# Turning two tensors on the matrix engine, keeping off-diagonal blocks on chip, and moving short transfers to ScalarE's queue, in a recurrent-attention and MLP kernel

## Chip, core and metric

The kernel runs on one core of a Trainium2 chip. Its engines have instruction streams of their own: TensorE (PE in the profile, PEld for its weight loads), VectorE (DVE), ScalarE (ACT), GpSimd (POOL) and SyncE (SP). SP here only issues DMA transfers. The metric is the device time of one execution in microseconds.

## The reference

A recurrence over 768 steps (4 batches of 8 heads, state 40x40), and two MLP layers on its result:

```python
for t in range(S):
    y[:, :, t] = np.einsum('bhd,bhde->bhe', rt, state)
    Sa = np.einsum('bhde,bhe->bhd', state, at)
    state_decay = state * wt[:, :, None, :] - np.einsum('bhd,bhe->bhde', Sa, bt)
    state = state_decay + np.einsum('bhd,bhe->bhde', vt, kt)
...
h = np.maximum(xt @ w_tok1, 0.0) @ w_tok2          # over tokens
u = x + h.transpose(0, 2, 1)
x = u + np.maximum(u @ w_ch1, 0.0) @ w_ch2         # over channels
...
ch = np.maximum(xn @ w_ch1, 0.0) @ w_ch2           # second layer, xn = layer-normed x
out = x + ch
```

MLP weights come in as float64 and are decoded from their bits on the chip.

## The kernel before

The 768 steps of a batch are cut into 12 chunks of 64. There are 48 chunks in all; two neighbours make a *pair* (24 pairs, `gi`), eight make a *group* (6 groups, `G`). Every fp32 value is split into a high and a low fp16 part, so a product is three matmuls (`T3`).

For each group the background steps are: `stack` loads b, a, k, v, r (tile `x`), scales them by running products of w (`sx`, `wf`), writes the two fp16 parts into `o16` (one buffer for all tensors and groups; ACT at L785, DVE or POOL at L789 and L787) and stores it to DRAM (`scr_*`, L704). `gram_load` (L809) reads a and b back by DMA transposes into `at` and `tt_b`, four of each in a group. `gram` multiplies them (L826); the diagonal 32x32 blocks go to `sab` and DRAM `l_d` (L836), the off-diagonal ones as high and low part to `lc` (L833, L834) and DRAM `o_d` (L838). `solve` reads `l_d` back as `ug` (L843), inverts 32x32 triangles by 60 dependent DVE steps (L853, L855), and stores the result `u16` to DRAM `t_d` (L867).

For each pair `pair_load` fetches k, v, r transposed (L926), rows (L929), and `tu` from `t_d` (L941). `low_load` fetches the off-diagonal blocks into `lx`, one 64-row buffer whose other half holds zeros (L951). `early` makes the scores of k and a, masks them, and forms the inverse's lower block: 48 matmuls of `lx` with `tu`, their result back into `lx`, then 48 more (L995). `chain` (twice for a pair) is the recurrence; it cannot start on a pair before `early` of it is done. `yout_a` and `yout_b` form the outputs. `split_mask` masks a 128x512 PSUM tile on DVE into SBUF (`se`, `sm`, L958), makes the high part on ACT (L961) and the low one on POOL (L962).

Weights: 56 pieces are loaded (`raw`, three buffers, L1135), decoded by four DVE steps (L1137 to L1144), scaled and split by ACT (L1159, L1162), and their low part formed by POOL (L1163). The MLP of a batch (L1240 token product; L1289, L1292 and L1299 channel products, L1246 and L1247 the split between them) can start when all 12 chunks of the batch are through.

The order on each engine is no hand's work: `fix_order` lists all instructions, simulates them with costs (`cost`, `mode`, `LAG`) and fixes the resulting order engine by engine. All DMAs stand in SP's queue.

Of the kernel before, what the change touches and what calls it, by code (L numbers as in the profile page):

```python
# [195 lines left out]
STAY = 1500  # L196
CLOCK = 4096 / 1.2
# [3 lines left out]
def cost(i, engine):  # L201
# [17 lines left out]
    if "Dma" in kind or "DMA" in kind:  # L219
# [5 lines left out]
        return 625 if len(rows) > 1 or 64 in rows or turned else 450, size / piece * (9 + piece / 27) / k  # L225
# [29 lines left out]
class Graph:  # L255
# [114 lines left out]
    def latest(self, key):  # L370
# [16 lines left out]
        while events:  # L387
# [5 lines left out]
            for e in engines:  # L393
# [4 lines left out]
                if move:  # L398
                    dma = max(now, dma) + move
                    begin[x] = dma + 650 + own  # L400
                    busy[e] = max(now + own + 25 + (545 if self.turns(x) else 0), dma - 1500)
                else:
                    begin[x] = busy[e] = now + own
# [11 lines left out]
    def schedule(self, rank):  # L415
# [22 lines left out]
        issue = dma = 0  # L438
        warm, window, active, tiles = False, 0, 0.0, 0
        port = dict(DVE=0, Pool=0)  # L440
        order = {e: [] for e in engines}
        events = [(0, 0, x) for x in range(n) if not wait[x]]
        heapq.heapify(events)
        while events:
# [7 lines left out]
            for e in engines:  # L452
# [35 lines left out]
                if move:  # L488
                    begin = max(now + 100, issue)
                    issue = begin + own + 25  # L490
                    dma = end = max(begin + own + 650, dma) + move
                    busy[e] = begin + own - 75 + (620 if self.turns(pick) else 0) if e == "SP" else begin + 900
# [49 lines left out]
def tile_main(  # L542
# [86 lines left out]
    lx = const.tile([128, 8, 2, 64], F16, name="lx")  # L629
# [33 lines left out]
    def zero_rings():  # L663
        for ring in (tt_r, [lx], n16_r, [zero]):
# [8 lines left out]
    l_d, t_d, o_d = {}, {}, {}  # L673
    for G in range(NG // TG):
# [5 lines left out]
        o_d[G] = dr.tile([2, 32, TG * NPAIR, 64], F16, name=f"o_d{G}")  # L680
# [25 lines left out]
    def pre_steps(G):  # L706
# [64 lines left out]
        def stack(n, src, e):  # L771
# [19 lines left out]
            store_lanes(scr[n, G], o16)  # L791
# [6 lines left out]
    def t_steps(G):  # L798
        TU = 8

        st_i = {}

# [9 lines left out]
        def gram(i):  # L812
            st = st_i[i]
            if G == 0:
                lc = chp.tile([128, TU, 2, 32], F16, name="lc", tag="sak", bufs=2)
                sab = chp.tile([128, TU, 32], F32, name="sab", tag="sm", bufs=2)
            else:
                lc = pre.tile([128, TU, 2, 32], F16, name="lc")
                sab = pre.tile([128, TU, 32], F32, name="sab")
            for j in range(TU // 4):  # L820
# [15 lines left out]
            nc.sync.dma_start(out=l_d[G].rearrange("(u l) t -> l u t", l=128)[:, TU * i:TU * i + TU, :], in_=sab)  # L836
            for h2 in range(2):
                nc.sync.dma_start(out=o_d[G][h2][:, TU * i:TU * i + TU, :],  # L838
                                  in_=lc[64 * h2:64 * h2 + 32].rearrange("p u r t -> p u (r t)"))

        def solve():
            ug = pre.tile([128, 32, 32], F32, name="ug")
            nc.sync.dma_start(out=ug.rearrange("p s t -> p (s t)"),  # L843
# [13 lines left out]
            for s0 in range(0, 32, 8):  # L857
# [9 lines left out]
                nc.sync.dma_start(out=dv[:, s0:s0 + 8, :], in_=u16.rearrange("p s r t -> p s (r t)"))  # L867
# [7 lines left out]

        return dict(gram=load + steps, solve=[solve])
# [42 lines left out]
    def pair_load(gi, late):  # L919
# [553 lines left out]
```

## Time and profile before

| | us |
|---|---|
| median of three runs | 1201.86 (1199.35 to 1214.21) |
| the profiled execution | 1205.77 |
| its span in the trace, first to last instruction | 1204.1 |

[...] A queue name with q (SPq) is the issuing part of an engine. "Idle before" is the idle time of an engine ahead of an instruction, with what ended it.

### The profile page before, as it was taken

Reading aid. Unit: us, or ns where it says so; the run is one execution under the profiler, and the core shown is the slowest. Engines: PE = TensorE matmul, PEld = TensorE weight load, DVE = VectorE, ACT = ScalarE, POOL = GpSimd, SP = SyncE. Lnnn points to the kernel's source line nnn. Section 1 sums busy time; section 2 is a strip of 40 time slices with the busy share of each in tenths; the row PEclk is TensorE's granted clock in tenths of the full one; section 3 lists DMA queues with packets and bytes.
Section 4 is the critical chain, followed back from the end, with each engine's and each line's share of the span. In section 5 each row is a group of like instructions: output and inputs, shape, how many; then the busy total and the mean of one; then the engine's idle time right before and its main releaser. Section 6 shows DMA issues by size and latency. Waiting matters only on the chain.

```text
span 1204.1 us, 37444 instructions
## 1 busy us (share of the span) xinstructions
PE 870.2 (72%) x15950; PEld 702.5 (58%) x15950; DVE 735.2 (61%) x1769; ACT 614.8 (51%) x1425; POOL 341.8 (28%) x340
## 2 busy tenths in 40 slices
PE   0010000456768668898989999889899999999997
PEld 0010000445657556676767777667778877788875
DVE  6866578678855774667854579536854453434432
ACT  1462228756777355853567634585474453332221
POOL 2765553552225522072231143121111001100000
PEclk9999999999999578998989999889999999999999
DMA  4899999797995899879899657977475554222111
GB/s 153 222 240 233 189 210 254 199 193 163 198 194 121 207 170 217 114 146 128 169 197 142 147 81 177 166 149 173 97 131 87 72 71 77 35 42 38 27 25 26
DMA packets 401726, 170.95 MB, mean 142 GB/s; under 512 B 370576, under 2 KB 381328, under 8 KB 397712
## 3 DMA queue, kind: packets, MB, share of 16 engines
q1 hardware_dynamic: 401552, 168.48, 70.2%
q8 instruction: 127, 2.08, 0.7%
q14 instruction: 47, 0.39, 0.1%
HBM read 73.27 MB, written 54.26 MB: 106 GB/s over the span
## 4 chain that ended last, share of the span: by engine, by line
PE 37%; ACT 8%; DVE 8%; DMA 7%; issue 3%; POOL 1%; SPq 1%; POOLq 0%; ACTq 0%; DVEq 0%
PE pb L1299 12%; PE pa L1289 10%; PE ch L907 4%; PE pa L1292 3%; PE ps L907 3%; DMA ut<-u 2%; DVE ug L855 2%; ACT sab L829 1%; ACT tt L987 1%; DMA t_d<-u 1%; DVE hh L1247 1%; DVE tmp L853 1%; PE ps L1240 1%; PE ps L995 1%; ACT o L785 1%
## 5 line engine op out<-in xcount | busy, mean ns | idle before, releaser
L1299 PE MATMUL pb<-c,hh 128*128 128x320 f16 x864 | 183.3, 301 | 1.2 <-DVE hh L1247 1.1
L1289 PE MATMUL pa<-ut,c 128*128 128x256 f16 x864 | 169.4, 283 | 8.9 <-DVE hh L1247 4.4
L1247 DVE SCALAR_TENSOR_TENSOR hh<-pa,hh 128x512 f16<-128x512 f32 x132 | 90.5, 687 | 138.4 <-ACT hh L1246 138.1
L1299 PEld LDWEIGHTS <-hh 128*128 128x128 f16 x1584 | 153.1, 99 | 33.1 <-DVE hh L1247 1.6
L1246 ACT ACTIVATE hh<-pa 128x512 f16<-128x512 f32 x132 | 78.3, 594 | 162.4 <-PE pa L1292 159.8
L1299 PE MATMUL pb<-d,hh 128*128 128x320 f16 x720 | 151.8, 306 | 0.0
L1289 PE MATMUL pa<-ut,d 128*128 128x256 f16 x720 | 141.1, 281 | 5.4 <-DMA ut<-u 4.4
L962 POOL TENSOR_TENSOR srx<-sm,srx 128x512 f16<-128x512 f32 x48 | 56.7, 1182 | 285.0 <-ACT srx L961 281.8
L1289 PEld LDWEIGHTS <-c 128*128 128x128 f16 x864 | 86.2, 102 | 30.9 <-issue 4.6
L1289 PEld LDWEIGHTS <-d 128*128 128x128 f16 x720 | 70.9, 101 | 25.8 <-DMA ut<-u 3.4
L855 DVE TENSOR_TENSOR ug<-ug,tmp 128x30 f32<-128x30 f32 (+9 forms) x180 | 83.7, 465 | 1.6
L995 PE MATMUL ps<-tu,lx 64*64 64x32 f16 x2304 | 65.2, 190 | 26.2 <-DMA lx<-o_d 8.2
L785 ACT ACTIVATE o<-x 128x2560 f16<-128x2560 f32 x30 | 70.0, 2332 | 26.3 <-POOL x L712 17.3
L853 DVE TENSOR_TENSOR tmp<-ug 128x30 f32<-128x30 f32 (+9 forms) x180 | 81.3, 451 | 1.9
L826 PEld LDWEIGHTS <-tt_b 120*128 120x128 f16 x192 | 15.4, 117 | 111.5 <-issue 47.4
L826 PE MATMUL pa<-at,tt_b 120*128 120x128 f16 x64 | 8.2, 308 | 98.0 <-DMA at<-scr_a 39.1
L995 PEld LDWEIGHTS <-lx 64*64 64x64 f16 x2304 | 57.8, 123 | 34.4 <-issue 19.3
L1292 PE MATMUL pa<-ut,c1t 128*128 128x256 f16 x288 | 67.7, 281 | 0.0
L987 ACT ACTIVATE tt<-tu 32x512 f16<-32x512 f16 x96 | 60.1, 626 | 13.3 <-PE ch L907 10.7
L907 PEld LDWEIGHTS <-srx 64*64 64x64 f16 x2304 | 57.6, 121 | 13.8 <-issue 11.5
L1325 POOL TENSOR_TENSOR y<-ve,mhalf 128x2 f32<-128x2 f32 x12 | 9.0, 747 | 181.2 <-DVE ve L1323 123.6
L1140 DVE TENSOR_SCALAR wst<-raw 128x320 int32<-128x320 int32 (+2 forms) x56 | 33.9, 608 | 43.4 <-DMA raw<-in_moe_w_ch_dram 32.2
(195 smaller groups left out, 2031.8 us busy)
## 6 DMA issues: line engine op xcount, KB each, us to landing
raw<-in_moe_w_ch_dram SPq DMA_DIRECT2D x30, 320.0 KB
scr_b<-o SPq DMA_DIRECT2D x6, 1024.0 KB
scr_a<-o SPq DMA_DIRECT2D x6, 1024.0 KB
scr_k<-o SPq DMA_DIRECT2D x6, 1024.0 KB
scr_v<-o SPq DMA_DIRECT2D x6, 1024.0 KB
scr_r<-o SPq DMA_DIRECT2D x6, 1024.0 KB
t_d<-u SPq DMA_DIRECT2D x24, 256.0 KB
tu<-t_d SPq DMA_DIRECT2D x24, 256.0 KB
```

Source lines behind the costliest of these rows:

```text
L785: A.activation(out=hi2, in_=x.unsqueeze(2).broadcast_to([128, HC, 2, D]), func=ACTF.Copy, scale=p2(e))
L853: V.tensor_tensor(out=tv, in0=ug[:, 0:s, s:s + 1].broadcast_to([128, s, n]), in1=ug[:, s:s + 1, s + 1:32].broadcast_to([128, s, n]), op=AL ...
L855: V.tensor_tensor(out=ug[:, 0:s, s + 1:32], in0=ug[:, 0:s, s + 1:32], in1=tv, op=ALU.add)
L907: m = nc.tensor.matmul(out, lhsT, rhs, start=start, stop=stop, skip_group_check=True)
L962: P.tensor_tensor(out=o[:, 1], in0=sm, in1=o[:, 0], op=ALU.subtract)
L987: A.activation(out=tt[l0:l0 + 32, :, :, l0 % 64:l0 % 64 + 32], in_=d["tc"][l0:l0 + 32], func=ACTF.Copy)
L995: nc.tensor.matmul(pv[hs, u, :], lw[hs, u, l, :], rhs[hs, u, m, :], start=n == 0, stop=n == 2)
L1246: nc.scalar.activation(out=hi, in_=ps, func=ACTF.Relu)
L1247: nc.vector.scalar_tensor_tensor(out=lo, in0=ps, scalar=0.0, in1=hi, op0=ALU.max, op1=ALU.subtract)
L1289: nc.tensor.matmul(o, w1[:, f, l, ms], ut[:, f + 3 * q, :], start=n == 0, stop=False)
L1292: nc.tensor.matmul(o, w1t[:, ms], ut[:, 2 + 3 * q, :], start=False, stop=q == 1)
L1299: nc.tensor.matmul(pb[i][:, 0:DM], hh[:, l, c0:c0 + 128], w2[:, m0 + s, q, :], start=m0 + s == 0 and n == 0, stop=m0 + s == nm - 1 and n == 2)
```

## The change

For groups 0 and 1 a and b are no longer read back by DMA transposes: a new step `turn` turns `o16` on PE (32 transposes of 128x120 for each tensor), and ACT and DVE copy the result, eight copies each, into `at` and, for b, into the weight tile `d2`, which is not yet in use. a of these groups is not stored at all. `lc` gets six buffers and is read directly by `early`, so that `o_d`, `lx` and `low_load` are gone; the two rounds of matmuls work on 32x32 tiles. The transfers of `l_d`, `ug`, `t_d` and `tu` (78 in all) are issued by ACT. `split_mask` masks in place in PSUM, and DVE makes the low part. The low part of decoded weights is made by DVE too. Planner: two queues, dearer transposes, a class for 32x32 tiles, and a rule that waits for more urgent work, with limits of zero.

```diff
+WAIT, GAP = 0, 0
-    return (rows <= 64) + 2 * (cols <= 64)
+    return (rows <= 64) + (rows <= 32) + 3 * ((cols <= 64) + (cols <= 32))
...
-    lx = const.tile([128, 8, 2, 64], F16, name="lx")
+    zx = const.tile([128, 8, 2, 32], F16, name="zx")
...
-            store_lanes(scr[n, G], o16)
+            if n != "a" or G > 1:
+                store_lanes(scr[n, G], o16)
...
+        def turn(n):
+            dst = []
+            for i in range(4):
+                st = st_i.setdefault(i, {})
+                if n == "a":
+                    st[n] = stk.tile([128, TU * 128], F16, name="at", bufs=NA)
+                    st_t.setdefault(4 * G + i, {})["a"] = st[n]
+                else:
+                    st[n] = wt["d2"].rearrange("p m l c -> p (m l c)")[:, i * TU * 128:(i + 1) * TU * 128]
+                dst.append(st[n][0:120].rearrange("p (l t) -> p t l", t=HC))
+            for t0 in range(0, HC, 8):
+                pt = ps_b.tile([128, 1024], F16, name="pb", tag="b")[0:120]
+                for t in range(8):
+                    nc.tensor.transpose(pt[:, t * 128:(t + 1) * 128], o16[:, t0 + t, 0:120], ident)
+                pv = pt.rearrange("p (t l) -> p t l", l=128)
+                for i in range(4):
+                    if i % 2:
+                        V.tensor_copy(dst[i][:, t0:t0 + 8], pv[:, :, 32 * i:32 * i + 32])
+                    else:
+                        A.activation(out=dst[i][:, t0:t0 + 8], in_=pv[:, :, 32 * i:32 * i + 32], func=ACTF.Copy)
...
-            nc.sync.dma_start(out=l_d[G].rearrange("(u l) t -> l u t", l=128)[:, TU * i:TU * i + TU, :], in_=sab)
-            for h2 in range(2):
-                nc.sync.dma_start(out=o_d[G][h2][:, TU * i:TU * i + TU, :],
-                                  in_=lc[64 * h2:64 * h2 + 32].rearrange("p u r t -> p u (r t)"))
+            A.dma_start(out=l_d[G].rearrange("(u l) t -> l u t", l=128)[:, TU * i:TU * i + TU, :], in_=sab)
...
     def split_mask(ps, tag, bufs):
-        own = tag == "sak"
-        sm = chp.tile([128, 8, 64], F32, name="se" if own else "sm", bufs=1 if own else 2)
-        V.tensor_tensor(out=sm, in0=ps.rearrange("p (u t) -> p u t", t=64),
-                        in1=causal.unsqueeze(1).broadcast_to([128, 8, 64]), op=ALU.mult)
+        sm = ps.rearrange("p (u t) -> p u t", t=64)
+        V.tensor_tensor(out=sm, in0=sm, in1=causal.unsqueeze(1).broadcast_to([128, 8, 64]), op=ALU.mult)
         o = chp.tile([128, 2, 8, 64], F16, name=tag, bufs=bufs)
         A.activation(out=o[:, 0], in_=sm, func=ACTF.Copy)
-        P.tensor_tensor(out=o[:, 1], in0=sm, in1=o[:, 0], op=ALU.subtract)
+        V.tensor_tensor(out=o[:, 1], in0=sm, in1=o[:, 0], op=ALU.subtract)
...
-        for k, (rhs, dst, sc, rows) in enumerate(((d["uc"], lw, p2(-E_T), 32), (d["tc"], tt, p2(-E_LO), 0))):
+        for k, (lhs, rhs, dst, sc, r0, c0) in enumerate(((d["lc"], d["uc"], zx, p2(-E_T), 0, 0),
+                                                         (zx, d["tc"], tt, p2(-E_LO), 32, 32))):
...
-                    for h2 in range(2):
-                        hs = slice(64 * h2, 64 * h2 + 64)
-                        nc.tensor.matmul(pv[hs, u, :], lw[hs, u, l, :], rhs[hs, u, m, :], start=n == 0, stop=n == 2)
+                    for p0 in (0, 64):
+                        ks, os = (slice(p0 + r, p0 + r + 32) for r in (r0, 32 - r0))
+                        nc.tensor.matmul(pv[os, u, :], lhs[ks, u, l, :], rhs[ks, u, m, :], start=n == 0, stop=n == 2)
...
-            P.tensor_tensor(out=lo, in0=f[p0:128], in1=hi[p0:128], op=ALU.subtract)
+            V.tensor_tensor(out=lo, in0=f[p0:128], in1=hi[p0:128], op=ALU.subtract)
...
-    run(bg(0, "w")[1:] + bg(0, "b a"))
+    run(bg(0, "w")[1:] + bg(0, "b tb a ta"))
```

The new order on SP's queue at the opening, from the store of group 0's b to the store of its k. Before (`scr_b`, `scr_a`, `scr_k` are DRAM copies of `o16`, `raw` are weights):

```order
L704 DMA scr_b_121<-o_118 128x4096
...
L809 DMA_TRANSPOSE tt_b<-scr_b_121 128x1024 x2
L1135 DMA raw<-in_moe_w_tok_dram 128x768
L938 DMA yw<-scr_y_124 128x8x40
L701 DMA wf<-in_w_dram 64x1x1280
L704 DMA scr_a_119<-o_118 128x4096
L701 DMA x<-in_r_dram 64x1x1280
...
L809 DMA_TRANSPOSE at<-scr_a_119 128x1024 x2
L701 DMA x<-in_r_dram 64x1x1280
L809 DMA_TRANSPOSE at<-scr_a_119 128x1024
```

Now, on the same queue:

```order
L722 DMA scr_b_121<-o_118 128x4096
L719 DMA x<-in_k_dram 64x1x1280
L722 DMA scr_y_124<-wf 128x1280
L719 DMA x<-in_k_dram 64x1x1280
L1165 DMA raw<-in_moe_w_tok_dram 128x768
L978 DMA yw<-scr_y_124 128x8x40
L719 DMA x<-in_r_dram 64x1x1280
L1165 DMA raw<-in_moe_w_tok_dram 128x768
L719 DMA wf<-in_w_dram 64x1x1280
```

The transposes and the store of a are gone, and the loads of r, v and the weights stand closer to the front.

On ACT, at the end of group 2's solve (`u` is the solved triangle, `tt` its copy for the matmuls). Before, with `t_d` and `tu` in SP's queue:

```order
L864 ACTIVATE u_4109<-ug 128x8x32 x2
L597 ACTIVATE o_118,stats<-x 128x4x40
L785 ACTIVATE o_118<-x 128x32x80
L1246 ACTIVATE hh<-pa 128x512 x2
L829 ACTIVATE sab<-ps 32x128 x4
L833 ACTIVATE lc<-ps 32x4x32
L987 ACTIVATE tt_111<-tu 32x16x32
```

Now, on ACT itself:

```order
L904 DMA t_d_142<-u_4231 128x1024
L904 DMA t_d_142<-u_4237 128x1024
L1081 ACTIVATE r_8433<-ch 128x160
L1130 ACTIVATE nmt<-ps 120x512
L1257 ACTIVATE x_11803<-xt 128x160
L981 DMA tu<-t_d_142 128x8x128 x2
L1130 ACTIVATE nmt<-ps 120x512
L616 ACTIVATE o_118,stats<-x 128x4x40
L803 ACTIVATE o_118<-x 128x32x2x40
L1017 ACTIVATE tt_111<-tu 32x16x32 x3
```

Stores and loads now stand in ACT's own stream, with three instructions between the last store and the load that needs it.

On DVE in the opening, around the a of group 0 (`pb` is the PSUM tile of the transposes, `d_181` the tile `d2`):

```order
L730 TENSOR_TENSOR x<-x,wf 128x1280
L839 COPY d_181<-pb 120x8x32 x2
L1174 SCALAR_TENSOR_TENSOR wst<-raw,wst 128x256
L1170 TENSOR_SCALAR wst<-raw 128x256
L1167 SCALAR_TENSOR_TENSOR bits<-raw,bits 128x256
L1172 SCALAR_TENSOR_TENSOR wst<-raw,wst 128x256
L1193 TENSOR_TENSOR t_167<-wst,t_167 128x256
L807 SCALAR_TENSOR_TENSOR o_118<-x,o_118 128x32x40
L839 COPY d_181<-pb 120x8x32
L730 TENSOR_TENSOR x<-x,sx 128x1280
```

The copies (L839) and the low parts of weights (L1193) are new rows on this engine. Up to the first `u` of group 0's solve, 31 weight pieces were decoded ahead of it before and 32 are now.

## Rows read from the trace of the kernel before

**Rows 1.** The page: busy us, share of the span, instructions, for each engine.

```profile
PE 870.2 (72%) x15950; PEld 702.5 (58%) x15950; DVE 735.2 (61%) x1769; ACT 614.8 (51%) x1425; POOL 341.8 (28%) x340
```

**Rows 2.** Busy us by window: length; PE, PEld, DVE, ACT, POOL; clock, DMA share, GB/s.

```profile
0.00:50.00 50.00, 2.12 (x12) 1.62 (x12) 38.00 (x94) 12.52 (x19) 25.43 (x40) 1.00 0.61 176
50.00:205.00 155.00, 12.55 (x192) 10.37 (x193) 107.00 (x209) 69.88 (x167) 77.66 (x74) 1.00 1.05 225
205.00:420.00 215.00, 137.78 (x3505) 118.96 (x3505) 151.32 (x339) 144.56 (x337) 93.72 (x88) 0.92 0.83 184
420.00:500.00 80.00, 63.18 (x1063) 47.99 (x1063) 51.38 (x130) 47.45 (x111) 16.74 (x15) 0.87 1.01 179
500.00:900.00 400.00, 361.60 (x7091) 286.11 (x7091) 262.67 (x661) 240.65 (x574) 109.06 (x105) 0.94 0.78 146
900.00:1204.00 304.00, 292.92 (x4091) 237.49 (x4089) 124.80 (x340) 99.70 (x220) 19.18 (x19) 0.99 0.30 50
```

**Rows 3.** Waits of PE, 0 to 205 us: us, times, longest.

```profile
PE pa L826 <- DMA at<-scr_a: 39.1, 2, 28.2
...
PE ps L975 <- DMA kt<-scr_k: 37.6, 4, 15.2
```

**Rows 4.** SP's issue of the transposes, 0 to 205 us: ns min/median/max.

```profile
L809 SPq DMA_TRANSPOSE tt_b<-scr_b x8: 1165/2191/4227, 41.0 to 192.7; - x8
L809 SPq DMA_TRANSPOSE at<-scr_a x8: 1172/2720/4989, 54.7 to 163.9; - x8
```

**Rows 5.** DVE groups, 0 to 205 us: busy, mean ns, idle before with its releasers.

```profile
L1142 DVE SCALAR_TENSOR_TENSOR wst<-raw,wst 128x384 int32<-128x384 int32 x16 | 14.0, 876 | 0.0
L1140 DVE TENSOR_SCALAR wst<-raw 128x384 int32<-128x384 int32 x16 | 11.6, 726 | 25.2 <-DMA raw<-in_moe_w_ch_dram 22.8 <-POOL sx L712 2.1 <-DMA x<-in_k_dram 0.3
L1140 DVE TENSOR_SCALAR wst<-raw 128x320 int32<-128x320 int32 x12 | 9.7, 817 | 9.2 <-DMA raw<-in_moe_w_ch_dram 8.1 <-POOL c L1163 1.1
L1144 DVE SCALAR_TENSOR_TENSOR wst<-raw,wst 128x384 int32<-128x384 int32 x16 | 9.7, 606 | 0.1
L1140 DVE TENSOR_SCALAR wst<-raw 128x256 int32<-128x256 int32 x6 | 1.9, 325 | 6.9 <-DMA raw<-in_moe_w_tok_dram 6.9
```

**Rows 6.** SP's queue at the end of group 0's solve: start, duration.

```profile
191.78 0.33 SPq L867 DMA_DIRECT2D t_d<-u  x1
...
202.79 0.54 SPq L867 DMA_DIRECT2D t_d<-u  x1
...
206.77 1.07 SPq L941 DMA_DIRECT2D tu<-t_d  x2
```

**Rows 7.** Waits of PE, 205 to 420 us.

```profile
PE ps L995 <- DMA lx<-o_d: 7.8, 4, 3.2
```

**Rows 8.** PE blocks in order of time: start, duration, tile, count.

```profile
235.30 0.61 PE L907 MATMUL ch<-vx,kb 64*40 64x40 f16 x24
235.74 1.44 PE L995 MATMUL ps<-tu,lx 64*64 64x32 f16 x48
237.02 0.81 PE L907 MATMUL ch<-r,tt 64*64 64x40 f16 x24
...
776.57 0.93 PE L995 MATMUL ps<-tu,lx 64*64 64x32 f16 x48
```

**Rows 9.** DVE groups, 500 to 900 us, and the page's POOL row.

```profile
L958 DVE TENSOR_TENSOR sm<-ps,causal 128x512 f32<-128x512 f32 x21 | 14.4, 687 | 8.2 <-PE ps L975 7.8
L1000 DVE SCALAR_TENSOR_TENSOR lx<-ps,lx 32x256 f16<-32x256 f32 x23 | 9.7, 424 | 8.8 <-ACT lx L999 7.8
...
L962 POOL TENSOR_TENSOR srx<-sm,srx 128x512 f16<-128x512 f32 x48 | 56.7, 1182 | 285.0 <-ACT srx L961 281.8
```

**Rows 10.** The chain of waits: start, length, what.

```profile
441.70 11.71 DMA ut<-u
...
596.01 6.87 DMA t_d<-u
...
663.70 9.13 DMA l_d<-sab
```

More of the change, by code (lines that the diff above doesn't have):

```diff
@@ L224, in cost @@
         k = 16 if turned else max(q for q in range(1, 17) if all(n % q == 0 for n in outer(aps)))
-        return 625 if len(rows) > 1 or 64 in rows or turned else 450, size / piece * (9 + piece / 27) / k
+        return 625 if len(rows) > 1 or 64 in rows or turned else 450, size / piece * (9 + piece / 27) / k * (1.6 if turned else 1.05)
     if engine == "PE":
@@ L398, in latest @@
                 if move:
-                    dma = max(now, dma) + move
-                    begin[x] = dma + 650 + own
-                    busy[e] = max(now + own + 25 + (545 if self.turns(x) else 0), dma - 1500)
+                    if e == "SP":
+                        dma = max(now, dma) + move
+                        begin[x] = dma + 650 + own
+                        busy[e] = max(now + own + 25 + (545 if self.turns(x) else 0), dma - 1500)
+                    else:
+                        begin[x] = now + 2 * move + 650 + own
+                        busy[e] = now + own + 25
                 else:
@@ L437, in schedule @@
         busy = dict.fromkeys(engines, 0)
-        issue = dma = 0
+        issue, queue = dict.fromkeys(engines, 0), dict.fromkeys(engines, 0)
         warm, window, active, tiles = False, 0, 0.0, 0
         port = dict(DVE=0, Pool=0)
+        soon = dict(DVE=[], Activation=[])
         order = {e: [] for e in engines}
@@ L481, in schedule @@
                     heapq.heappush(avail[e], q)
+                if pick is not None and e in soon:
+                    soon[e] = [q for q in soon[e] if q[0] > now]
+                    if any(t < now + WAIT and rank[y] > rank[pick] + GAP and self.cost[pick][0] > t - now for t, y in soon[e]):
+                        heapq.heappush(avail[e], (-rank[pick], pick))
+                        pick = None
                 if pick is None:
@@ L488, in schedule @@
                 if move:
[L489 to L492, printed above, removed]
+                    begin = max(now + 100, issue[e])
+                    issue[e] = begin + own + 25
+                    other = queue["SP" if e != "SP" else "Activation"]
+                    end = max(begin + own + 650, queue[e])
+                    shared = min(move, max(0, other - end))
+                    end += move + shared
+                    queue[e] = end
+                    if other > end:
+                        queue["SP" if e != "SP" else "Activation"] += move
+                    busy[e] = begin + own - 75 + (620 if self.turns(pick) else 0)
                 else:
@@ L663, in zero_rings @@
     def zero_rings():
-        for ring in (tt_r, [lx], n16_r, [zero]):
+        for ring in (tt_r, n16_r, [zero]):
             for t in ring:
@@ L672, in tile_main @@
     scr = {}
-    l_d, t_d, o_d = {}, {}, {}
+    l_d, t_d = {}, {}
     for G in range(NG // TG):
@@ L874, in t_steps @@
             steps.append(lambda i=i: gram(i))
+        if G < 2:
+            return dict(ta=[lambda: turn("a")], tb=[lambda: turn("b")],
+                        gram=[lambda i=i: gram(i) for i in range(n)], solve=[solve])
         return dict(gram=load + steps, solve=[solve])
@@ L1381, in attend @@
                 early(i + 1)
-                if i + 2 < NG // 2:
-                    low_load(i + 2)
             if i > 0:
@@ L1402, in tile_main @@
     run(bg(0, "k v r y"))
-    run(bg(1, "b a gram solve k v r y"))
+    run(bg(1, "b tb a ta gram solve k v r y"))
     run(wtodo)
```

34 lines of the change are left out of this document (13 added, 21 removed).

## The prediction

> **What bounds the kernel now.** I read the page's busy times first, then the busy time by stage, then the waits of each stage. Over the whole span no engine is full: PE, the busiest, has 72% [rows 1]. The stages tell more [rows 2]. From 900 us on PE is busy 292.9 of 304 us, from 500 to 900 us 361.6 of 400. So from 500 us on the time is PE's work, and only some 50 us are idle. In the first 205 us PE does nearly nothing: 2.1 and 12.6 us. That is the reserve. Work that PE could take up earlier shortens the kernel about one for one, as long as PE stays full afterwards.
>
> The opening ends when the first triangles arrive (`tu`), so that `early` and the recurrence can run. Until then PE waits 39.1 us for turned a and 37.6 us for turned k [rows 3]. The DMA share is 1.05 from 50 to 205 us [rows 2], and DVE stands idle for weight loads 22.8 + 8.1 + 6.9 = 37.8 us [rows 5]. So the opening is bound by transfers, with DVE next: 38.0 + 107.0 = 145 us busy of 205. From 205 to 420 us nothing is full (PE 64%, DVE 70%, ACT 67%); there the recurrence's own latency counts. From 420 to 500 us the DMA share is 1.01 again.
>
> The sum is made against the profiled execution's own time, 1205.8 us (its span is 1204.1); the median of the three runs lies 3.9 us lower, and I take that off at the end.
>
> **Turning a and b of two groups (the opening).** Sixteen transposes go. What one costs the DMA engines no row shows; SP spends 2.2 to 2.7 us on issuing one [rows 4], so 8 x 2.2 + 8 x 2.7 = 39 us bound it from above, and from below 16 x 256 KB at the stage's 225 GB/s [rows 2], 19 us. Two stores of 1 MB go too: 2 x 4.7 = 9 us at that rate. So 28 to 48 us of transfer time leave the opening. DVE's 37.8 us of waiting for weights shrink by about as much, and I take all 37.8. Against this DVE gets new work ahead of the first solve's end. Some 32 low parts of weights come from POOL; their nearest row is the three-operand weight step at 606 ns [rows 5], so 32 x 0.6 = 19 us. About 28 copies out of PSUM, nearest row 424 ns for 256 elements [rows 9], are 12 us. POOL in turn has less to do, and it slows DVE: the same kind of step took 876 ns in one place and 606 ns in the other [rows 5]. Sixteen such steps at 0.27 us less are 4.3 us; over all widths and steps I take 8 back (0 to 14). Net: 37.8 + 8 - 19 - 12 = 15 us. The 128 transposes on PE lie in its idle time and cost nothing; without that cover they would be about 128 x 0.1 = 13 us.
>
> **Short transfers on ACT's queue.** After the first solve SP issued the four `t_d` stores between 191.8 and 202.8 us, with other work of its queue between them, and `tu` at 206.8 [rows 6]. On ACT the stores follow the splits directly. Of the 15 us I take 11 as gained for the first pairs (0 if DVE delivers the last `u` as late as now). Opening together: 15 + 11 = 26 us earlier, between 8 (DVE fills what the transfers leave) and 45 (all transfer time counts).
>
> Queued behind the waiting issues on ACT are the evacuations for the recurrence and the MLP, and PE waits for those. The order leaves three instructions between the last `t_d` store and the load that needs it. Stores took 6.9 us and `l_d` 9.1 us where they stood on the chain [rows 10]. Each group has two such places; but before, ACT waited at `tt` for the same `tu`. I take +6 us over all groups, between 0 and 25.
>
> [...]
>
> **Off-diagonal blocks kept in SBUF.** The 7.8 us that PE waits for `lx` before 420 us [rows 7] go; the pairs are latency-bound there, so I count 8 (0 to 11; waits for the second half of `lx` remain as waits for `zx`). Later these loads hide behind PE's other work: 0.
>
> The 32x32 matmuls: a block of 48 takes 1.44 us in the opening and 0.93 us at 776 us [rows 8]. A block of 24 with 64 stationary columns takes 0.81 us there, with 40 columns 0.61 [rows 8], so fewer columns are cheaper, by up to a quarter. A quarter of 0.93 us on the 34 later blocks is 8 us; the ends of the blocks don't shrink, so I take 5 (0 to 8). Some 25 more changes of tile shape stand in PE's order; blocks that follow each other in one shape overlap by 0.17 us at their ends [rows 8], and if a change of shape loses that, 25 of them cost 4; I take 2 (0 to 4).
>
> [...]
>
> **Masks in PSUM, low parts on DVE.** 72 subtractions go from POOL (1182 ns) to DVE, where the mask itself takes 687 ns [rows 9]: 72 x 0.69 = 50 us of DVE, of which 18 x 0.69 = 12 lie from 205 to 420 us, with some 24 weight parts of 0.5 us, 12 more. DVE has 64 us idle there [rows 2], so most is hidden; a recurrence step that finds DVE busy waits, and I take +4 (0 to 22; 22 to 24 if the cover were gone). After 500 us DVE is idle 137 of 400 us: 0. A PSUM bank is held some 2 us longer for each mask, off the recurrence.
>
> **420 to 500 us.** The first MLP block waits 11.7 us for its transposed input behind a full DMA [rows 10]. With a shorter backlog I take 4 of it (0 to 11.7).
>
> **Sum.** 26 + 8 + 5 + 4 = 43 off; 6 + 2 + 4 = 12 on; 31 net. 1205.8 - 31 = 1174.8, and less 3.9 gives **1171 us**.
>
> **Rivals.** *Transfers set all of the opening.* DVE's new work hides in what it waits now. Then the opening gives 45 instead of 26 and the first MLP block all 11.7: 1171 - 19 - 8 = 1144. For it: DMA share 1.05 and DVE's waits. Against: with the waits gone DVE would be 93% busy or more.
>
> *DVE becomes the bound of the opening.* It is busy 145 of 205 us now; with 31 us more and 8 less it needs 168, and its order mixes solve steps with weight steps that wait for loads. Then the opening gives 8, and the recurrence to 420 us pays 15 instead of 4: 1171 + 18 + 11 = 1200. A planner that misjudges its new costs would look the same.
>
> *The change doesn't do what it says:* gram's a may come no earlier, since its copies share ACT and DVE with weight work. Then the opening gives 0: 1197; I put it with the case before.
>
> *Slower: ACT stands at its own transfers.* In each group ACT meets `l_d` to `ug` and `t_d` to `tu`, 9.1 + 6.9 = 16 us at the rows' price [rows 10], 6 x 16 = 96 us in all. MLP blocks need ACT for every 128x512 split, so PE would stop with it. It decides if more than 60 of the 96 us reach PE; with 64 of them in place of my 6 the time is 1171 + 58 = 1229. Against it: other ACT work stands between, and PE holds other matmuls.
>
> **How the numbers follow.** Two per cent is about what a measurement of this kernel can tell from no change: 1178 and 1226. My forecast 0.42 (1150 to 1192), transfers alone 0.22 (1125 to 1150), DVE bound or no gain at the start 0.26 (1190 to 1215), ACT stalls 0.10 (1215 to 1260). Faster by over 2%: 0.22 and 0.7 of 0.42, 0.51. Slower: most of 0.10, with a little of the DVE case, 0.10. Same: 0.39. The range 1130 to 1212 leaves out the slow case and the ends of the others.
>
> **What would show it.** Right: L1026 (32x32 matmuls) starts near 180 us in place of 205; DVE's idle time before L1170 falls under 10 us by then and DVE is over 85% busy; no wait for `lx`; a 48 block at 0.7 to 0.93 us late in the run; PE stays over 90% busy from 470 us on. Wrong: L1026 starts at 200 us or later with DVE full (the DVE rival); ACT's waits for DMA at L904, L981 and L880 sum to over 40 us with PE idle beside them (the slow rival); or the start is early and the MLP still begins at 420 us, held by its weights.

## The result, and the profile after

The changed kernel takes **1221.18 us** (median of 15 runs, 1215.22 to 1229.56), beside 1204.9 us for the kernel before (15 runs): ratio 1.0134, 95% interval 1.0104 to 1.0163. That is under 2%, but it is a loss, and it lies above the range of the prediction (1130 to 1212). The profiled execution took 1229.56 us; it was the longest of the fifteen.

The page, busy us of each engine, after:

```profile
PE 875.1 (71%) x16078; PEld 702.2 (57%) x16078; DVE 788.1 (64%) x1928; ACT 650.5 (53%) x1457; POOL 209.2 (17%) x212
```

Against [rows 1], DVE has 52.9 us more, ACT 35.7 more, and POOL 132.6 less. By stage (columns as in [rows 2]; the clock is the granted TensorE clock as a share of its full speed, the DMA share the mean busy share of the core's 16 DMA engines):

```profile
0.00:50.00 50.00, 7.13 (x52) 6.18 (x53) 36.08 (x95) 20.05 (x23) 8.19 (x21) 1.00 0.50 151
50.00:205.00 155.00, 21.24 (x235) 17.19 (x233) 115.42 (x227) 83.23 (x146) 64.50 (x58) 1.00 0.60 164
205.00:420.00 215.00, 116.02 (x3130) 99.55 (x3132) 164.41 (x390) 148.83 (x360) 43.52 (x41) 1.00 0.83 179
420.00:500.00 80.00, 54.63 (x1057) 42.64 (x1056) 53.39 (x126) 40.45 (x93) 17.10 (x12) 0.82 0.92 177
500.00:900.00 400.00, 362.26 (x6992) 283.61 (x6989) 272.81 (x707) 239.98 (x571) 71.73 (x74) 0.95 0.79 146
900.00:1228.00 328.00, 313.77 (x4624) 253.02 (x4622) 145.97 (x385) 118.01 (x268) 4.21 (x6) 0.99 0.30 53
```

The transfers did leave the opening: from 50 to 205 us the DMA share fell from 1.05 to 0.60. Nothing came earlier for it. Up to 205 us PE is busy 13.7 us longer, with the 128 new transposes (17.0 us, 0.13 us each). From 205 to 420 us PE does 21.8 us less than before, from 420 to 500 us 8.6 less, and at 500 us it has 362.26 + 313.77 = 676.0 us of work left where it had 654.5. That is 21.5 us, and the trace's span is 23.8 us longer. So the loss is made before 500 us.

DVE's groups from 0 to 205 us (busy, mean ns, idle before with its releasers), those that answer to [rows 5], the turned copies, and low parts of weights:

```profile
L839 DVE COPY d<-pb 120x256 f16<-120x256 f16 x16 | 19.7, 1298 | 8.1 <-ACT d L841 7.1 <-ACT wct L769 1.0
L839 DVE COPY at<-pb 120x256 f16<-120x256 f16 x13 | 16.3, 1272 | 0.0
...
L1193 DVE TENSOR_TENSOR c<-wst,c 128x384 f16<-128x384 f32 x8 | 4.7, 591 | 10.1 <-ACT c L1192 10.1
...
L1170 DVE TENSOR_SCALAR wst<-raw 128x320 int32<-128x320 int32 x8 | 2.8, 346 | 13.3 <-DMA raw<-in_moe_w_ch_dram 13.3
...
L1170 DVE TENSOR_SCALAR wst<-raw 128x256 int32<-128x256 int32 x6 | 1.7, 283 | 7.5 <-DMA raw<-in_moe_w_tok_dram 7.5
```

A copy of 256 halves (fp16 values) per partition takes 1.27 to 1.30 us, not the 0.424 us that I took from [rows 9]. ACT's half of the copies is as slow:

```profile
L841 ACT ACTIVATE d<-pb 120x256 f16<-120x256 f16 x16 | 20.0, 1371 | 13.5 <-PE pb L835 7.1 <-DVE d L839 5.0 <-DVE wf L730 1.3
L841 ACT ACTIVATE at<-pb 120x256 f16<-120x256 f16 x15 | 18.7, 1352 | 10.4 <-PE pb L835 8.6 <-DVE at L839 1.6
```

And the engines' queues stand behind each other. Each engine's instructions run in the planned order, and one that waited held those behind it, on ACT for 12.9 us here. ACT, in order of time from 101 us (idle before in brackets):

```profile
101.40 0.37 ACTq L876 DMA_DIRECT2D l_d<-sab  x1
...
102.37 0.52 ACT L1192 ACTIVATE c<-wst 128x384 f16<-128x384 f32 x1
115.39 0.34 ACTq L880 DMA_DIRECT2D ug<-l_d  x1
115.78 0.52 ACT L1189 ACTIVATE wst<-wst 128x384 f32<-128x384 f32 x1 [12.89 <-DMA l_d<-sab]
```

`ug` waits for the last `l_d`, ACT's weight steps stand behind that issue, and DVE's low part at L1193 stands 10.1 us for one of them. The first 32x32 matmuls wait for `tu` until 242.5 us; before, the first triangles came at 210.1 us. One line of the kernel before, then two of the changed one:

```profile
210.09 1.46 PE L995 MATMUL ps<-tu,lx 64*64 64x32 f16 x48 [7.03 <-DMA tu<-t_d]
```

```profile
242.54 0.82 PE L1026 MATMUL ps<-tu,lc 32*32 32x32 f16 x48 [12.36 <-DMA tu<-t_d]
...
1026.34 0.76 PE L1026 MATMUL ps<-tu,lc 32*32 32x32 f16 x48
```

### The profile page after: what moved, and what is told of

Read it like the earlier page. It is cut to its first block, busy times and chain, and to the rows that moved or that the text cites. A ratio compares the mean times of both kernels' runs of the same rounds, so it can differ in the third digit from the quotient of the medians.

```text
span 1227.9 us, 37463 instructions
## 1 busy us (share of the span) xinstructions
PE 875.1 (71%) x16078; PEld 702.2 (57%) x16078; DVE 788.1 (64%) x1928; ACT 650.5 (53%) x1457; POOL 209.2 (17%) x212
## 4 chain that ended last, share of the span: by engine, by line
PE 37%; DVE 10%; issue 10%; ACT 9%; DMA 8%; SPq 1%; POOL 1%; ACTq 0%; another core or an unknown queue 0%; POOLq 0%; DVEq 0%
PE pb L1329 12%; PE pa L1319 9%; PE ch L947 5%; PE pa L1322 3%; PE ps L947 3%; ACT o L803 2%; ACT tt L1017 1%; DMA tu<-t_d 1%; DMA t_d<-u 1%; DVE ug L892 1%; PE pb L947 1%; DMA x<-in_r_dram 1%; PE ps L1270 1%; ACT sab L869 1%; DVE hh L1277 1%
## 5 line engine op out<-in xcount | busy, mean ns | idle before, releaser
L1329 PE MATMUL pb<-c,hh 128*128 128x320 f16 x864 | 176.2, 302 | 0.0
L1319 PE MATMUL pa<-ut,c 128*128 128x256 f16 x864 | 163.3, 281 | 7.4 <-issue 5.1
L1355 POOL TENSOR_TENSOR y<-ve,mhalf 128x2 f32<-128x2 f32 x12 | 8.6, 720 | 446.8 <-DVE stats L1351 242.5
L892 DVE TENSOR_TENSOR ug<-ug,tmp 128x30 f32<-128x30 f32 (+9 forms) x180 | 76.8, 427 | 2.2
L890 DVE TENSOR_TENSOR tmp<-ug 128x30 f32<-128x30 f32 (+9 forms) x180 | 62.5, 347 | 5.8 <-POOL ug L884 4.1
L866 PE MATMUL pa<-at,d 120*128 120x128 f16 x64 | 9.2, 308 | 73.9 <-DVE lc L874 71.4
L835 PE MATMUL pb<-ident,o 128*120 128x128 f16 x128 | 17.0, 318 | 60.9 <-POOL o L805 24.0
L947 PEld LDWEIGHTS <-srx 64*64 64x64 f16 x2304 | 53.4, 124 | 10.1 <-issue 7.1
L805 POOL TENSOR_TENSOR o<-x,o 128x1280 f16<-128x1280 f32 x15 | 46.9, 3125 | 69.6 <-ACT o L803 51.1
L947 PEld LDWEIGHTS <-kb 64*40 64x40 f16 x2112 | 41.2, 102 | 26.6 <-issue 25.6
L989 DVE TENSOR_TENSOR ps<-ps,causal 128x512 f32<-128x512 f32 x60 | 41.4, 692 | 22.8 <-PE ps L1005 21.0
L1322 PE MATMUL pa<-ut,d1t 128*128 128x256 f16 x240 | 55.7, 277 | 0.0
```

The source lines that it names most:

```text
L805: P.tensor_tensor(out=o16[:, :, lo:lo + D], in0=x, in1=o16[:, :, 0:D], op=ALU.subtract)
L890: V.tensor_tensor(out=tv, in0=ug[:, 0:s, s:s + 1].broadcast_to([128, s, n]), in1=ug[:, s:s + 1, s + 1:32].broadcast_to([128, s, n]), op=AL ...
L892: V.tensor_tensor(out=ug[:, 0:s, s + 1:32], in0=ug[:, 0:s, s + 1:32], in1=tv, op=ALU.add)
L947: m = nc.tensor.matmul(out, lhsT, rhs, start=start, stop=stop, skip_group_check=True)
L989: V.tensor_tensor(out=sm, in0=sm, in1=causal.unsqueeze(1).broadcast_to([128, 8, 64]), op=ALU.mult)
L1319: nc.tensor.matmul(o, w1[:, f, l, ms], ut[:, f + 3 * q, :], start=n == 0, stop=False)
```

## The experiments

Three theories of the loss were tried: that the work put on DVE and ACT costs (W), that the new order of the in-order queues does (O), and that the late stages do (L). A planner sets the order, so every edit gives another order too; the last runs ask how much that alone is worth. Ratios are to the kernel before on the same chip.

| kernel | median us | ratio, 95% interval | first triangles, us |
|---|---|---|---|
| before | 1204.90 | 1 | 210 |
| changed | 1221.18 | 1.0134, 1.0104 to 1.0163 | 242 |
| e1 copies in runs | 1194.07 | 0.9888, 0.9858 to 0.9918 | 212 |
| e2 short on SP | 1225.24 | 1.0126, 1.0062 to 1.0190 | 261 |
| e3 no turn | 1190.13 | 0.9847, 0.9782 to 0.9912 | 190 |
| e4 low on POOL | 1221.53 | 1.0116, 1.0051 to 1.0181 | 237 |
| e5 copies priced | 1209.24 | 1.0050, 1.0013 to 1.0088 | 220 |
| e6 runs, short on SP | 1195.89 | 0.9932, 0.9893 to 0.9972 | 240 |
| e7 no turn, short on SP | 1183.43 | 0.9835, 0.9781 to 0.9888 | 203 |
| e8 kept blocks, masks | 1186.88 | 0.9883, 0.9829 to 0.9937 | 214 |
| e9 e7, few transposes | 1185.04 | 0.9840, 0.9735 to 0.9945 | 202 |
| e10 runs, priced | 1185.02 | 0.9826, 0.9738 to 0.9915 | 206 |
| e11 one group turned | 1204.68 | 0.9996, 0.9952 to 1.0039 | 193 |
| e12 e7, other order | 1197.44 | 0.9912, 0.9873 to 0.9952 | 202 |
| e13 before, few transposes | 1227.47 | 1.0205, 1.0162 to 1.0248 | 248 |
| e14 changed, other order | 1217.40 | 1.0106, 1.0067 to 1.0146 | 232 |
| e15 runs, other order | 1198.11 | 0.9938, 0.9905 to 0.9971 | 219 |
| e16 before, other order | 1219.33 | 1.0116, 1.0057 to 1.0175 | 228 |

**e1: the copies write in runs.**

```diff
-dst.append(st[n][0:120].rearrange("p (l t) -> p t l", t=HC))
+dst.append(st[n][0:120].rearrange("p (l t) -> p l t", t=HC))
-pv = pt.rearrange("p (t l) -> p t l", l=128)
+pv = pt.rearrange("p (t l) -> p l t", l=128)
-V.tensor_copy(dst[i][:, t0:t0 + 8], pv[:, :, 32 * i:32 * i + 32])
+V.tensor_copy(dst[i][:, :, t0:t0 + 8], pv[:, 32 * i:32 * i + 32])
```

> The changed kernel, with the 64 copies of turned a and b out of PSUM walking their elements in the other order: they write runs of 8 neighbouring halves (16 bytes) in place of single halves 64 bytes apart, and read PSUM with the stride instead. Same amount of work otherwise. Theory W (work): the opening is later because the turned copies and the weight parts put more on DVE and ACT than they had room for; a copy took 1.27 us on DVE and 1.30 us on ACT where I had priced 0.42. If the strided write is the cause, a copy now takes 0.5 us (0.4 to 0.8), DVE and ACT each lose some 24 us in the opening, the first 32x32 matmul moves from 242 us to about 222 us and the time from 1221 to about 1205 us. Rival O (order): the in-order queues wait for each other (SP for a buffer of x, ACT for its own short transfers), and the amount of work matters little: copies shorter, first 32x32 matmul at 242 us within 8, time 1221 within 6. Rival L (late): the loss is in the stages after 420 us, from the 32x32 tiles and DVE's low parts: the start moves as in W, the time stays over 1215. If the copies stay at 1.27 us, the strided write is not the cause.

The same two groups of DVE, from 0 to 205 us, in e1:

```profile
L839 DVE COPY at<-pb 120x256 f16<-120x256 f16 x16 | 6.6, 416 | 0.0
...
L839 DVE COPY d<-pb 120x256 f16<-120x256 f16 x16 | 6.2, 415 | 2.7 <-ACT d L841 2.7
```

And ACT's:

```profile
L841 ACT ACTIVATE d<-pb 120x256 f16<-120x256 f16 x16 | 5.9, 381 | 14.1 <-PE pb L835 9.7 <-DVE d L839 4.4
L841 ACT ACTIVATE at<-pb 120x256 f16<-120x256 f16 x16 | 5.8, 378 | 9.6 <-PE pb L835 8.6 <-DVE at L839 0.8
```

0.416 us is nearly the 0.424 that I had priced. 32 copies on DVE at 0.86 us less are 27 us, 32 on ACT at 0.98 less 31, and the kernel is 27 us faster. So it is the write that costs: the slow order reads 32 neighbouring halves of PSUM and writes them 64 bytes apart; the fast one reads 256 bytes apart and writes 8 neighbouring halves. I had not weighed the step of the writes; what makes it cost is not shown by two orders. W is confirmed for the copies, and by more than I had put (1205). L is not: the copies all lie before 230 us, and the time fell under the 1215 that L had set.

By stage, e1 from 50 to 500 us:

```profile
50.00:205.00 155.00, 20.76 (x244) 16.92 (x245) 120.97 (x262) 77.86 (x188) 55.22 (x60) 1.00 0.71 192
205.00:420.00 215.00, 135.38 (x3625) 115.88 (x3626) 166.23 (x401) 143.53 (x338) 46.54 (x43) 0.99 0.88 178
420.00:500.00 80.00, 63.69 (x1050) 47.69 (x1045) 41.48 (x101) 51.00 (x132) 7.12 (x9) 0.75 0.83 151
```

PE has its 19.4 and 9.1 us back. But the triangles come at 212 us, as before the change, with the DMA share at 0.71: my 26 us of earlier start are missing even at my own price for the copies.

**e2, e6 and e7: the short transfers on SP again**, in the changed kernel, in e1 and in e3.

```diff
-            A.dma_start(out=l_d[G]...
+            nc.sync.dma_start(out=l_d[G]...
```

(Likewise `ug`, `t_d` and `tu`.)

> The changed kernel with its short transfers (l_d, ug, t_d, tu) issued by SP again, in all six groups; nothing else undone. Theory W: ACT's 12.9 us behind ug go, the transfers pay some waits in SP's queue instead; first 32x32 matmul from 242 to about 232 us, time about 1212 us. Rival O: these issues are one of the places where queues meet; ACT's stop goes and SP's own stops grow, time 1205 to 1230 with no relation to the work moved. My own slower rival of the prediction (ACT stands at its transfers in all groups) would give 1200 or less. Rival L: within 5 us of 1221.

> The kernel with copies in runs of 8 halves (start at 212 us, time 1194), with its short transfers issued by SP again. Theory S (ACT's stop behind its own ug, 13.4 us, with DVE 11.8 us behind it, holds the start): start at 200 to 204 us, time 1186. Rival Q (SP's queue pays more than ACT does: the issues then stand behind buffers of x and of raw weights): start at 215 to 230 us, time 1196 to 1205.

> The kernel without turned copies (DMA transposes, start at 190 us, time 1190), with its short transfers issued by SP again. If ACT's queue is what brought the start from 210 us (before) to 190 us, it goes back to 203 to 210 us and the time to 1200 or more. If it was the low parts on DVE and the kept blocks, the start stays at 190 us within 5 and the time at 1190 within 5.

Three pairs: 1.0134 and 1.0126, 0.9888 and 0.9932, 0.9847 and 0.9835. In none do the intervals part. Moving the short transfers gives nothing and costs nothing that can be measured, although with them on SP the first triangles come 13 to 28 us later. That e6 starts at 240 us and ends with e1, which starts at 212, is the plainest sign that the start of the first triangles does not set the time.

**e3: no turn.** The first two groups go through DMA transposes again.

```diff
-            if n != "a" or G > 1:
-                store_lanes(scr[n, G], o16)
+            store_lanes(scr[n, G], o16)
...
-        if G < 2:
-            return dict(ta=[lambda: turn("a")], tb=[lambda: turn("b")],
-                        gram=[lambda i=i: gram(i) for i in range(n)], solve=[solve])
...
```

> The changed kernel with a and b of the first two groups turned by DMA transposes again (16 transposes and two more stores of 1 MB); short transfers on ACT, kept blocks, 32x32 tiles, masks in PSUM and low parts on DVE stay. Theory W: the opening is bound by transfers again as before the change (first triangles at 205 to 210 us), DVE has its low parts in the time that it waits; first 32x32 matmul at 215 us (205 to 225), time 1204 us (1195 to 1212). Rival O: DVE and ACT keep standing behind each other, start at 235 us or later, time over 1212. Rival L: start near 210 us as before the change and the time still over 1215, since what costs lies behind 420 us.

It is 31 us faster than the changed kernel, more than W or either rival had given. The DMA share from 50 to 205 us is 1.01 again, and the triangles come at 190 us, the earliest of all: full DMA engines and the earliest start stand together.

**e4: weights' low parts on POOL again.**

```diff
-            V.tensor_tensor(out=lo, in0=f[p0:128], in1=hi[p0:128], op=ALU.subtract)
+            P.tensor_tensor(out=lo, in0=f[p0:128], in1=hi[p0:128], op=ALU.subtract)
```

> The changed kernel with the low parts of the weights on POOL again; all else stays. Theory W: DVE loses some 32 x 0.5 = 16 us in the opening and gets part of it back as longer steps beside POOL; first 32x32 matmul from 242 to about 232 us, time 1212 us (1206 to 1220). Rival O: POOL holds x of SP's loads longer, and the start stays at 242 us or moves later; time 1221 or more. Rival L: DVE's low parts after 205 us are what costs; the start stays within 5 us, the time falls to 1212 or less.

1.0116 beside 1.0134: no difference, and the start moves by 5 us. None of the three theories gets its number.

**e5 and e10: the planner knows the price.** Its formula takes 0.14 us on DVE and 0.26 on ACT for a copy.

```diff
+    if aps[0].bass_ap.tensor.space == PSUM and "16" in str(aps[0].dtype) and aps[0].ap[0][1] == 120 and engine != "PE":
+        return (1270 if engine == "DVE" else 1290), 0
```

> The changed kernel, its 64 turned copies as slow as they are (single halves 64 bytes apart), but the planner is told their measured price, 1.27 us on DVE and 1.29 us on ACT, where its formula gives 0.14 and 0.26 us. Theory W (the copies' own time on DVE and ACT costs): an order that knows the price can do little, first 32x32 matmul at 242 us within 8, time 1221 within 6. Rival P (the order was planned with a wrong price, and that costs): the order gets round the copies, start at 220 us or earlier, time 1204 or less.

> The kernel with turned copies in runs of 8 halves (1194 us), and the planner is told their measured prices, 414 ns on DVE and 383 ns on ACT, where its formula gives 137 and 263. If what the turn still costs against DMA transposes lies in an order planned too cheaply, time 1186 us or less; if the work itself makes up for the transfers that it saves, 1194 us within 6.

e5 lies between the two theories: by the ratios it is 10 us faster than the changed kernel. e10 (414 and 383 ns) is 7 us faster than e1. Both lie within what order alone does (below), so that the price did it is not shown.

**e8: two parts alone on the kernel before** (from the changed kernel: no turn, short transfers on SP, the weights' low parts on POOL, old DMA prices).

```diff
...
-size / piece * (9 + piece / 27) / k * (1.6 if turned else 1.05)
+size / piece * (9 + piece / 27) / k
...
```

> The kernel before with only two parts of the change: gram's blocks kept in SBUF with 32x32 tiles, and the scores masked in PSUM with their low parts on DVE (the two need each other's room in SBUF). DMA transposes, short transfers on SP, the weights' low parts on POOL and the planner's old DMA prices as before. By the terms of my sum: waits for lx 8 off, 32x32 tiles 5 off, tile changes 2 on, some DVE load 2 on, so 9 under before, about 1196 us (1190 to 1205), start at 205 to 212 us. If these parts gave all of what the kernel without turned copies gains, 1190 us or less; if they cost, over 1210 us.

0.9883, 14 us under the kernel before, where my terms said 9. e7, which adds DVE's low parts of weights and the planner's new transfer prices, has 0.9835. So these parts could be nearly all of what the kernels without the turn gain; but order alone moves the kernel before by 14 us too (e16), so it is not shown that they are.

**e9 and e13: 12 of the 16 transposes left out**, in e7 and in the kernel before.

```diff
+            if G < 2 and i:
+                st["a"], st["b"] = st_i[0]["a"], st_i[0]["b"]
+            else:
...
```

> The kernel without turned copies and with short transfers on SP (start at 203 us, time 1183, DMA share 1.05 from 50 to 205 us), with 12 of the 16 DMA transposes of the first two groups left out: all four tiles of such a group use the turned a and b of its first tile, so these pairs' values are not the reference's. Nothing takes the place of the 12. Theory T (my prediction's: the opening is bound by transfers; its terms put 16 transposes at 19 to 39 us): 14 to 29 us earlier, start at 175 to 189 us, time 1155 to 1169. Theory D (DVE's own work paces the opening, and transfers wait beside it): start and time within 6 us of 203 and 1183, the DMA share falls under 0.9.

> The kernel before the change, with 12 of the 16 DMA transposes of its first two groups left out (all four tiles of such a group use the turned a and b of its first tile, so these pairs' values are not the reference's). Nothing takes their place. Theory T (the prediction's: the opening is bound by transfers, and 16 transposes are 19 to 39 us of them): first matmul of the triangles at 181 to 196 us instead of 210, time 1175 to 1190. Theory D (DVE's chain of solve and weights paces it): start at 210 us within 8, time 1204 within 8, DMA share well under 1.

Neither is faster; e13 is 2% slower. From 50 to 205 us, e13:

```profile
50.00:205.00 155.00, 11.51 (x180) 9.06 (x180) 99.33 (x202) 65.98 (x134) 97.27 (x90) 1.00 0.86 207
```

DVE's waits there, 0 to 205 us (us in total, times, longest):

```profile
DVE wst L1143 <- DMA raw<-in_moe_w_ch_dram: 25.2, 7, 6.9
DVE wst L1143 <- DMA raw<-in_moe_w_tok_dram: 18.5, 3, 8.1
```

43.7 us of waits for weights in e13, against 37.8 before, with 12 transposes gone. In e9 they are 29.9 us, in e7 16.2. So leaving the transposes out did not shorten these waits. Order blurs the times: a gain at the low end of theory T's 14 to 29 us could hide in e9, but e13 lies above both orders of the kernel before. e9 met what theory D had said (202 us, 1185 us, DMA share 0.86); e13 missed D as well (248 us, 1227 us).

What PE waited for at `gram` (L826 before), from 0 to 260 us, tells more. The kernel before, then e13:

```profile
PE pa L826 <- DMA at<-scr_a: 39.1, 2, 28.2
PE pa L826 <- DVE lc L834: 38.6, 3, 29.6
```

```profile
PE pa L829 <- DVE lc L837: 93.5, 6, 66.3
PE pa L829 <- DMA at<-scr_a: 21.4, 2, 16.2
```

The second line is one that [rows 3] passes over. PE waited for DVE's `lc` (L834, the step that reads the PSUM tile `pa`) as long as for the turned a, and with 12 transposes gone the wait for DVE grew by more than the other shrank. In the changed kernel, without transposes in these groups, it is 71.4 us.

What paces the loads of weights was not tried by itself; in the changed kernel SP's queue shows one such place, in order of time:

```profile
165.28 0.33 SPq L1165 DMA_DIRECT2D raw<-in_moe_w_ch_dram  x1
179.82 1.15 SPq L719 DMA_DIRECT2D x<-in_v_dram  x2
```

For 14 us SP holds at a load of x whose buffer POOL still reads, and the loads of weights stand behind it. The same trace shows POOL's step and who stands behind it, POOL first, then DVE:

```profile
169.97 9.83 POOL L805 TENSOR_TENSOR o<-x,o 128x1280 f16<-128x1280 f32 x1 [9.49 <-ACT o L803]
```

```profile
176.94 0.40 DVE L890 TENSOR_TENSOR tmp<-ug 128x238 f32<-128x238 f32 x1
190.59 0.33 DVE L1170 TENSOR_SCALAR wst<-raw 128x320 int32<-128x320 int32 x1 [13.26 <-DMA raw<-in_moe_w_ch_dram]
190.83 0.40 DVE L892 TENSOR_TENSOR ug<-ug,tmp 128x238 f32<-128x238 f32 x1
```

POOL's step, 2.61 us in the median of its fifteen, takes 9.83 us here, beside an unbroken run of DVE steps (spans on POOL are rough). SP's load follows at its end, the weights behind that at 181.57 us, and DVE stands for 13.3 us with the next step of the first solve (L892) behind a weight step in its order. This is one place in one execution; what it costs in time was not tried.

**e11: only the first group turned.**

```diff
-            if n != "a" or G > 1:
+            if n != "a" or G > 0:
-        if G < 2:
+        if G < 1:
```

> Only the first group's a and b turned by PE, with copies in runs of 8 halves at their measured prices; the second group by DMA transposes; short transfers on SP; the rest as in the changed kernel. If PE's turn brings the first solve forward where nothing else waits, and the second group's transposes hide behind it, the start is at 190 us or earlier and the time at 1176 us or less, the fastest of all. If DVE paces the opening, the copies cost what the transfers gave: 1183 to 1194 us.

1204.68, slower than e7 (no group turned) and e10 (both), and above both of my expectations, with the first triangles at 193 us.

**e12, e14, e15 and e16: the same instructions, another order.**

```diff
-STAY = 1500
+STAY = 1200
```

> The kernel without turned copies and with short transfers on SP (1183 us), with one number of the planner changed: PE may leave the most urgent matmul for one of the same tile shape up to 1200 ns of urgency away, in place of 1500. The instructions are the same and only their order differs. It is a control: by how much the time moves when nothing but the order does. I expect 1183 us within 6; a larger change would mean that differences of half a per cent between the other kernels say nothing about their parts.

> The changed kernel with the planner's 1500 set to 1200: the same instructions, another order. If the loss of the change is the slow copies' work, the time stays at 1221 us within 10 and stays over every kernel with copies in runs. If it was an unlucky order, 1205 us or less.

> The kernel with copies in runs of 8 halves and the planner's 1500 set to 1200. If the 27 us between it and the changed kernel are the copies' speed, 1194 us within 10, and 15 us or more under the changed kernel with the same 1200. If they were the order, the two come together.

> The kernel before with the planner's 1500 set to 1200; only the order differs. I expect the time within 10 us of 1204, and the granted clock of PE to differ by stage where the time does (in the control run it was 0.80 in place of 0.98 from 205 to 420 us and 14 us were lost).

Nothing but order moves the ratio by 0.0077 (e7 to e12) and by 0.0116 (before to e16), more than I had expected of either, and by 0.0028 and 0.0050 for the other two, as expected. Two windows of e7, then of e12:

```profile
205.00:420.00 215.00, 140.40 (x3673) 119.84 (x3674) 156.93 (x377) 143.55 (x337) 50.24 (x43) 0.98 0.89 182
500.00:900.00 400.00, 363.38 (x7276) 289.35 (x7274) 268.70 (x702) 244.56 (x579) 70.81 (x73) 0.92 0.74 144
```

```profile
205.00:420.00 215.00, 138.95 (x3593) 118.75 (x3594) 153.21 (x364) 138.46 (x325) 48.81 (x43) 0.80 0.88 177
500.00:900.00 400.00, 368.33 (x7123) 291.74 (x7124) 275.51 (x695) 238.86 (x573) 68.88 (x73) 0.89 0.72 142
```

The granted clock is 0.80 in place of 0.98 in one stage (a mean; in the trace of the kernel before it is 1.00 from 300 to 380 us and 0.50 from 387 to 420); in the stage from 500 us PE is busy 5 us longer and issues fewer matmuls. By itself the clock does not explain the times. In ten executions of e6, with one order, the mean clock of the run was 0.933 to 0.938 six times, with 1189.37 to 1202.06 us, and 0.967 to 0.975 four times, with 1197.05 to 1202.03 us. In e12 it ran from 0.919 to 0.959, and the three executions at 0.957 or more took 1193.06 to 1200.55 us. e16, 14 us slower than the kernel before, has 1.00 from 205 to 420 us where that has 0.92, and 0.88 from 500 to 900 us where that has 0.94. How an order makes a kernel slower stays open.

So a difference of 1% between two kernels here tells nothing about a part; families do. Slow copies: 1.0134, 1.0126, 1.0116, 1.0106, 1.0050. Runs: 0.9888, 0.9932, 0.9938, 0.9826. They don't overlap, and their means are 0.0210 apart, 25 us. Pair by pair (changed and e1, e2 and e6, e14 and e15, e5 and e10) the difference is 0.0246, 0.0194, 0.0168 and 0.0224. No turn: 0.9847, 0.9835, 0.9912, mean 0.9865, 4 us under the runs, which is nothing here. The kernel before: 1 and 1.0116. The changed kernel in its two orders lies inside or just above what the kernel before does in its two.

## Why the prediction was wrong

**What bounds the kernel.** That the time from 500 us on is PE's work held. One window from 500 us to the end, changed kernel, then e1, then e7:

```profile
500.00:1228.00 728.00, 676.03 (x11614) 536.63 (x11610) 418.78 (x1092) 357.99 (x838) 75.94 (x80) 0.97 0.57 104
```

```profile
500.00:1193.00 693.00, 644.07 (x11098) 511.92 (x11096) 399.39 (x1052) 331.45 (x766) 75.29 (x80) 0.97 0.57 104
```

```profile
500.00:1184.00 684.00, 637.37 (x11007) 510.35 (x11003) 393.47 (x1034) 336.18 (x784) 74.96 (x79) 0.95 0.54 104
```

PE is idle 52, 49 and 47 us there, and 49.5 before [rows 2]. The time is 500 us, plus PE's work left, plus about 50 (44 to 58 over all eighteen kernels).

**"So the opening is bound by transfers"** is the step that failed. I read it from a DMA share of 1.05 and DVE's waits for weights. That share says that transfers were under way all the time, not that the next stage waited for them. Taking 12 of 16 transposes away left the time where it was (e9) or made it worse (e13), and DVE's 37.8 us of waits, which I let vanish, were 20.8 in the changed kernel and 43.7 in e13. With the copies at my own price, e1's first triangles came at 212 us, not 26 us before 210. What the runs show in its place is PE's wait for DVE's `lc`, as long before as the one for turned a, 93.5 us in e13 and 71.4 in the changed kernel. It is no measure of the time either: e6 has 106.8 us of it and takes 1196. What bounds the opening instead stays open. My DVE rival (1200) does not fit as it stands: DVE was busy 181 of the first 242 us, so it was late without being full. A second part of the same step failed with it: I took the start of the first triangles as a measure of the gain. Starts of 190, 203, 212 and 240 us (e3, e7, e1, e6) go with 1190, 1183, 1194 and 1196 us.

**The copies (12 us on DVE)** were mis-sized. In the first 205 us they took 36.0 us on DVE and 38.7 on ACT, whose half I had put with nothing. My row of 0.424 us had the right count of elements and another write pattern. This term alone is some 25 us of the result (20 to 30 by the pairs): without it the kernel is at 1194, inside my range though not for my reasons. The 23 us from there to my 1171 are about as much as the 26 that the opening did not give.

**Low parts on DVE:** 28 in the first 205 us at 411 to 591 ns where I took 32 at 606; putting them back changes nothing (e4).

**POOL's slowing of DVE (8 us back):** the 64 decode steps of 128x384 took 49.1 us in the first 205 us before and 45.2 after, 3.9 less. The slowing itself is seen in the changed kernel: DVE steps that took 0.55 and 0.54 us at 142 us took 2.76 and 2.56 us at 152.46 and 155.15 us, beside POOL steps of 2.72 and 2.32 us that began at 152.28 and 154.97.

**Short transfers:** the 11 us gained did not come. ACT's waits for `l_d`, `t_d` and `tu` grew from 13.6 to 32.1 us over the run (12.9 of them in one stop) where I had put 6 us; in e2 they are 8.1 and the time is the same. My slower rival gave 1229, near the result, by this mechanism. e2 rules it out: ACT without its transfers gives 1225. The near hit was chance.

**Kept blocks:** the 7.8 us of waits for `lx` are gone, and waits for `zx` are 0.8 us in the whole run. A block of 48 takes 0.82 us early and 0.76 late, against 1.44 and 0.93 [rows 8]: 34 blocks at 0.17 are 6 us, and I had 5. The row served well: the two late blocks, 0.93 and 0.76 us, differ at the same free size of 32.

**Masks in PSUM:** PE's waits for DVE's masked scores stay under 8 us after 420 us; hidden there, as said. A masked tile is held 1.6 us longer in the median, from the mask's end (L989) to that of its low part (L992). From 205 to 420 us, where I had put 4 us, PE's waits for the recurrence's own DVE steps (`sas`, `n`, `r`) grew from 22.8 to 34.1 us, but over the kernels with masks in PSUM they lie between 19 and 37 (e8, e1), so this term is neither confirmed nor refuted.

**420 to 500 us:** the MLP's first product starts at 486.5 us where it started at 453.5 before; the 4 us of its wait can't be read off.

**The "no gain at the start" rival (1197)** described the kernel with fast copies, e1, at 1194; it lacked the copies' price. What the order of the queues added to the loss stays open between 0 and some 14 us, since that is what order alone does.

## What to carry to other kernels

Price a copy by what it writes as well as by its size: look for a row with the same step in memory, and if none is there, bound it by several times the nearest row (three here, 1.27 us beside 0.424) and try the other loop order first. A DMA share near 1 (1.05 here) is a bound only if the stage ends when transfers do; follow the chain from the end, read every long line of the waits, and count the work left for the engine that is full later, not the start of one instruction. Where a planner orders everything, give each kernel a second order before a difference of a per cent is laid to a part.

## What had not been expected of the hardware

Halves written 64 bytes apart cost 5.0 ns each per partition on DVE and 5.1 on ACT (medians of 1.27 and 1.30 us for 256); in runs of 8 they cost 1.6 and 1.5 ns (0.415 and 0.38 us), although PSUM is then read 256 bytes apart. The granted clock was 0.80 in e12 where it was 0.98 in e7 over 215 us, and its mean over whole runs differed between executions of one kernel (0.933 to 0.975 in e6) without the times following it. Where POOL and DVE ran side by side in the changed kernel, a DVE step of 0.55 us took 2.76 us, and a POOL step of 2.61 us took 9.83.
